# Where an attention kernel decodes the first dense layer's weights: four operations per engine in each of blocks 1 to 4, and dense products from block 5 on

## The chip, the core and the metric

One core of a Trainium2 chip runs the whole program. The metric is the device time of one execution in microseconds. The engines of the core run their own queues in order and meet through semaphores: TensorE (PE) multiplies and transposes, VectorE (DVE), ScalarE (ACT) and GpSimd (POOL) work on elements, SyncE (SP) issues the transfers.

## The reference, cut to what matters

The weight matrices arrive as float64 and reach the chip as raw 64-bit words. Three stages follow each other:

```python
# 1. attention, 2 batches x 8 heads, 768 positions, 64 per head; only 8 global keys and 96 local ones are kept
scores = q @ k.T / sqrt(64) - slope[h] * dist;  scores = where(keep, scores, -1e9)
x = softmax(scores) @ v                       # -> (2, 768, 512)
# 2. gated layer
h = relu(x @ w_in);  u, v = h[..., :512], h[..., 512:]
v_n = (v - mean(v)) / sqrt(var(v) + 1e-6)
v_s = w_spatial @ v_n + b_spatial             # over the 768 positions
x = (u * v_s) @ w_out
# 3. mixing layer
y = x + (x.T @ U @ V).T
out = y + relu(y @ w_ch1) @ w_ch2
```

## The kernel before

The kernel keeps everything of one batch in SBUF as two float32 halves, a rounded value (hi) and what is left (lo), and forms each product of the dense layers from three matmuls (`mm3`: hi hi, hi lo, lo hi).

The attention is a loop over `g`, the blocks of 128 queries: 12 of them (`NBL`), blocks 0 to 5 for the first batch and 6 to 11 for the second, and two more rounds to drain. It is pipelined over three rounds: block `g` computes its scores on PE (`em_s`), adds the bias on DVE (`em_soft`, which also finds the maximum), takes the exponential on ACT (`em_exp`) and scales on POOL (`em_norm`); the probabilities of block `g - 1` are transposed on PE (`em_t`, copied out of PSUM by ACT for even pairs of heads and by DVE for odd ones); those of block `g - 2` are multiplied with the values (`em_pv`) and written to `X` as hi and lo (`em_x`). The four pairs of heads of a block are its four pair steps `r`. Block 0's scores are taken before the masks and the bias for later blocks are finished.

Dense work that doesn't need the attention any more is put between these steps. It stands in a list, `fillers`, and `fill(more)` (line 659) takes `more` entries from it at each pair step: none in blocks 0 to 3, one in blocks 4 to 10, four from block 11 on (line 519; `TWO`, line 468, is 10). An entry is one step of three matmuls: first the four steps of each of six row tiles of `x @ w_in` for the half called `v` (`s_m1_v`, 24 entries, accumulated over the four chunks `k` of 128 rows; entry `k` needs chunk `k` of the weights), added from block 2 on, one tile per block; then 48 steps of the spatial product (`s_m2`), added at the end of block `TWO - 1`. From that block on the transposes use one PSUM bank instead of two, since the spatial product uses the other. What is left of `fillers` when the loop ends is taken behind it, together with the first product of the second batch.

Everything on DVE, ACT, POOL and SP that only prepares such work (decoding the weights from 64-bit words, splitting into hi and lo, loading `w_spatial`, layer normalisation) is not written at a fixed place but in chains, and a planner decides where it goes. The planner (class `Plan`) keeps for each engine the time at which it would be free by prices of its own. At certain points the program calls `tick` (line 162): it goes through the chains and emits the next operation of each for which the engine is free within `ROOM` (400 ns) of PE's own time and which needn't wait for more than `STALL` (100 ns); while `plan.most` is 1 (during the attention), at most one for each engine in a call. `flush` emits chains at once, whatever the planner thinks. There are two calls of `tick` in a pair step: behind the transposes and at its end; and one in each dense step.

The decoding of `w_in`'s `v` half consists of four chains (`early_work`, line 671), one for each chunk of 128 x 512 weights: an Abs on ACT; a clamp, a shift and two merging steps on DVE (`decode`, line 276); a rounding on ACT to `win` hi; a subtraction on POOL to `win` lo (`splits`, line 264). Their raw words are loaded at the start, into `rawin`, `masks` and `stg`. The first dense step calls `flush(P["wv"])`, that is, whatever of the four chains has not been emitted by then goes out at that point. Behind these chains come the load of `b_spatial` and those of `w_spatial` with their splits, which the spatial product needs.

Three small DVE operations on the counts of global and local keys and four that set a flag (`o_counts`, `o_flag`) form a chain of their own that is added at the end of block 0. The flag tells whether a second, dense program has to run after the first; with these inputs it doesn't.

Of the kernel before, what the change touches and what calls it, by code (L numbers as in the profile page):

```python
# [40 lines left out]
ROOM, CALM, STALL = 400.0, 450.0, 100.0  # L41
# [24 lines left out]
class Plan:  # L66
# [92 lines left out]
        if not c.ops:  # L159
            self.chains.remove(c)  # L160

    def tick(self):
        now, more, count = self.free["T"], True, dict.fromkeys(LAG, 0)
        while more:
            more = False
            for c in sorted(self.chains, key=lambda c: c.calm):
                key = c.ops[0][0]
                if any(d.ops for d in c.after) or self.free[key] > now + (CALM if c.calm else ROOM):
                    continue
                if self.most and count[key] >= self.most:  # L170
                    continue
                self.probing = 0.0
                c.ops[0][1]()
                start, self.probing = self.probing, None
                if start <= max(now, self.free[key]) + STALL:
                    count[key] += 1
                    self.emit(c)
                    more = True
# [14 lines left out]
def kernel(ctx: ExitStack, tc: tile.TileContext, qk, qt, kn, vab, vn_, gl_,  # L193
# [11 lines left out]
    def body(dense, sb, pp):  # L205
        plan = Plan(nc)
# [141 lines left out]
        if not dense:  # L348
# [116 lines left out]
                                        op0=ALU.mult, op1=ALU.mult)  # L465


            TWO = 10

            def em_t(g, r):  # L470
                x, bk = prob(g, r), bank[7 if g < TWO - 1 and r % 2 else 4].rearrange("p (h c q) -> p h c q", h=2, c=2)
# [25 lines left out]
            def attention():  # L497
                for e in range(2):
                    o_load(0, e)[0][1]()
                o_vals(0)[0][1]()  # L500
                A.activation(out=sm[:, 12:13], in_=nc.const_aps.tensor(0.0, (128, 1)), func=AF.Exp)
                V.memset(bank[4], 0.0)
                V.memset(bank[7], 0.0)
                masks_before()
                make_identity(nc, ident)
                for e in range(2):
                    o_load(1, e)[0][1]()
                early_work([t_x11[:, 0:1536], t_x11[:, 1536:3072], t_x10[:, 1536:3072], stg[:, 0:1536]])
                o_vals(1)[0][1]()
                plan.most = 1  # L510
                masks_first()
                masks_second()
                masks_third()
                for h in range(5, 8):
                    bias_g(Bt, rel, mk, h)


                for g in range(NBL + 2):
                    more = 0 if g < 4 else 1 if g < TWO else 1 if g == TWO else 4
                    if g == NB:  # L520
                        second_x()
                    xs = None
                    if g < NBL:
                        for r in range(NP):
                            em_s(g, r)
                        if g + 2 < NBL:
                            for e in range(2):
                                o_load(g + 2, e)[0][1]()
                    if g >= 2:
                        em_pv(g - 2)  # L530
                        if g < NBL:
                            o_vals(g)[0][1]()
                        xs = em_x(g - 2)
                    if g < NBL:
                        if g == 0:
                            for h in range(2, 4):
                                o_bias(B0, d0, m1, h)[1]()
                        em_soft(g, 0)
                        em_exp(g, 0)
                    if 0 < g <= NBL:  # L540
                        em_norm(g - 1, 1)
                    if g < NBL:
                        em_soft(g, 1)
                        em_exp(g, 1)
                        if g == 0:
                            for h in range(4, 8):
                                o_bias(B0, d0, m1, h)[1]()
                    if xs:
                        xs[0]()
                    for r in range(NP):  # L550
                        if xs and r == 1:
                            xs[1]()
                        if 0 < g <= NBL:
                            em_t(g - 1, r)
                            tick()
                        fill(more)
                        if g < NBL:
                            if r < 2:
                                em_soft(g, 2 + r)
                                em_exp(g, 2 + r)  # L560
                            if r == 1:
                                em_norm(g, 0)
                        tick()
                    if g == 0:
                        for h in range(5):
                            o_bias(Bt, rel, mk, h)[1]()
                        plan.add([("V", f) for f in o_counts() + o_flag()])
                    if 2 <= g < NB + 2:
                        fillers.extend(s_m1_v(0, g - 2, 6))
                    if g == NBL - 1:  # L570
                        plan.most = 0
                    if g == TWO - 1:
                        fillers.extend(s_m2(0, 6))

# [473 lines left out]
```

## Time and profile before

| what | value |
|---|---|
| three timed runs | 540.84, 541.87, 541.72 us; median 541.72 |
| profiled execution | 541.09 us, span from first to last instruction 539.3 us |
| mean granted clock of PE | 0.982 of 2.4 GHz |
| busy in the span | PE 506.0 us, DVE 305.6, ACT 213.5, POOL 176.0 |
| transfers | 44.74 MB, 83 GB/s in the mean |

The profiled execution is 0.6 us below the median; what is worked out from its rows is set against its own time. In the page's slices (13.5 us each) a digit is the busy share in tenths, and the row of the granted clock says at which share of 2.4 GHz PE was allowed to run. Views used are: the slices of the page, the list of PE's waits, single engines in order of time, groups of instructions by shape, and the busy time of each engine in chosen stretches. Nearly all instructions have the planner's line, L56, so they are told apart by their tiles: `raw` are the inputs of the scores, `prob` the probabilities, `ptb` their transposes, `win` the weights of the first layer, `wsp` those of the spatial product, `sm` small numbers.

### The profile page before, as it was taken

Reading aid. Unit: us, or ns where it says so; the run is one execution under the profiler, and the core shown is the slowest. Engines: PE = TensorE matmul, PEld = TensorE weight load, DVE = VectorE, ACT = ScalarE, POOL = GpSimd, SP = SyncE. Lnnn points to the kernel's source line nnn. Section 1 sums busy time; section 2 is a strip of 40 time slices with the busy share of each in tenths; the row PEclk is TensorE's granted clock in tenths of the full one; section 3 lists DMA queues with packets and bytes.
Section 4 is the critical chain, followed back from the end, with each engine's and each line's share of the span. In section 5 each row is a group of like instructions: output and inputs, shape, how many; then the busy total and the mean of one; then the engine's idle time right before and its main releaser. Section 6 shows DMA issues by size and latency. Waiting matters only on the chain.

```text
span 539.3 us, 7978 instructions
## 1 busy us (share of the span) xinstructions
PE 506.0 (94%) x2916; PEld 447.9 (83%) x2916; DVE 305.6 (57%) x734; ACT 213.5 (40%) x513; POOL 176.0 (33%) x207
## 2 busy tenths in 40 slices
PE   5847999799989999999999999999999999999994
PEld 3636877689869999888989898998988989989893
DVE  8777788753589963498699777685131111011113
ACT  4865977632253311564453433423212122121220
POOL 5526756430134401140024424233133232332310
PEclk9886999999999999999999999999999999999999
DMA  8772563130221210431215423420020000000003
GB/s 304 252 217 78 160 237 97 46 112 1 65 92 40 61 52 1 157 97 60 79 28 205 157 89 146 137 97 1 0 105 13 1 1 1 1 0 1 0 3 122
DMA packets 13520, 44.74 MB, mean 83 GB/s; under 512 B 1568, under 2 KB 3744, under 8 KB 11424
## 3 DMA queue, kind: packets, MB, share of 16 engines
q1 hardware_dynamic: 13328, 44.14, 24.3%
q8 instruction: 25, 0.41, 0.3%
q14 instruction: 23, 0.19, 0.1%
q10 hardware_dynamic: 144, 0.00, 0.0%
HBM read 40.99 MB, written 3.15 MB: 82 GB/s over the span
## 4 chain that ended last, share of the span: by engine, by line
PE 79%; DVE 11%; ACT 5%; issue 2%; DMA 1%; POOL 1%; ACTq 0%; SPq 0%; DVEq 0%
PE bank L56 79%; DVE stg L56 3%; DVE sm L56 2%; DVE prob L56 1%; ACT prob L56 1%; DVE y L56 1%; ACT ptb L56 1%; DVE u L56 1%; DMA stg<-in_w_in_dram 1%; DVE vn L56 1%; DMA ni<-in_gl_dram 1%; ACT stg L56 1%; DVE bias L56 1%; DVE work L56 1%; ACT x L56 0%
## 5 line engine op out<-in xcount | busy, mean ns | idle before, releaser
L56 POOL TENSOR_TENSOR wch<-f,wch 128x512 fp32r<-128x512 f32 x64 | 86.3, 1368 | 213.2 <-ACT wch L56 213.2
L56 PE MATMUL bank<-wch,h 128*128 128x512 f32 x576 | 139.4, 396 | 0.0
L56 PE MATMUL bank<-x,wch 128*128 128x384 f32 x768 | 139.1, 336 | 0.0
L56 PEld LDWEIGHTS bank<-x,wch 128*128 128x128 f32 x768 | 134.5, 188 | 3.1
L56 PEld LDWEIGHTS bank<-wch,h 128*128 128x128 f32 x576 | 107.8, 188 | 23.3
L56 DVE SCALAR_TENSOR_TENSOR h<-bank,h 128x384 fp32r<-128x384 f32 x64 | 35.5, 555 | 141.5 <-ACT h L56 141.5
L56 ACT ACTIVATE h<-bank 128x384 fp32r<-128x384 f32 x64 | 31.5, 492 | 179.5 <-PE bank L56 179.5
L56 ACT ACTIVATE prob<-prob,sm 128x232 f32<-128x232 f32 (+1 forms) x96 | 44.4, 464 | 29.1 <-DVE sm L56 29.1
L56 PE MATMUL bank<-wsp,vn 128*128 128x384 f32 x288 | 54.7, 341 | 1.1 <-POOL vn L56 0.3
L56 POOL TENSOR_SCALAR prob<-prob,sm 128x232 f32<-128x232 f32 (+1 forms) x96 | 43.4, 470 | 36.4 <-ACT prob L56 24.2
L56 PEld LDWEIGHTS bank<-wsp,vn 128*128 128x128 f32 x288 | 49.2, 188 | 2.8 <-DVE u L56 0.9
L56 PE MATMUL bank<-win,x 128*128 128x512 f32 x144 | 41.4, 422 | 9.9 <-ACT win L56 8.4
L56 DVE TENSOR_SCALAR f<-f 128x512 f32<-128x512 f32 (+1 forms) x64 | 41.3, 683 | 9.5 <-ACT f L56 9.3
L56 DVE SCALAR_TENSOR_TENSOR f<-raw,f 128x512 int32<-128x512 int32 x64 | 43.9, 725 | 0.1
L56 PEld LDWEIGHTS bank<-win,x 128*128 128x128 f32 x144 | 26.3, 197 | 14.6 <-ACT win L56 8.7
L56 ACT ACTIVATE wch<-f 128x512 fp32r<-128x512 f32 x64 | 36.9, 625 | 1.0 <-DVE f L56 1.0
L56 PE MATMUL bank<-x,win 128*128 128x384 f32 x192 | 34.2, 337 | 2.2 <-ACT win L56 1.3
L56 PE MATMUL bank<-ident,prob 128*128 128x128 f32 (+1 forms) x176 | 28.9, 287 | 7.2 <-ACT ptb L56 5.7
L56 PEld LDWEIGHTS bank<-x,win 128*128 128x128 f32 x192 | 33.2, 188 | 2.9 <-ACT win L56 1.7
L56 PE MATMUL bank<-wo,x 128*128 128x512 f32 x144 | 35.3, 395 | 0.0
L56 PEld LDWEIGHTS bank<-ident,prob 128*128 128x128 f32 (+1 forms) x176 | 20.7, 140 | 16.0 <-POOL prob L56 7.2
L56 DVE CUSTOM_DVE_ANT_0 prob<-bank,bias 128x232 f32<-128x232 f32 (+1 forms) x96 | 31.7, 369 | 2.6 <-PE bank L56 2.6
(87 smaller groups left out, 499.2 us busy)
## 6 DMA issues: line engine op xcount, KB each, us to landing
raw<-in_w_ch_dram SPq DMA_DIRECT2D x16, 1024.0 KB, 4.8
raw<-in_qk_dram SPq DMA_DIRECT2D x20, 360.0 KB, 3.8
vals<-in_vab_dram SPq DMA_DIRECT2D x10, 512.0 KB, 4.3
out_dram<-y SPq DMA_DIRECT2D x12, 256.0 KB, 2.2
stg<-in_w_in_dram SPq DMA_DIRECT2D x5, 512.0 KB, 5.9
stg<-in_w_sp_dram SPq DMA_DIRECT2D x3, 768.0 KB, 4.5
stg<-in_w_out_dram SPq DMA_DIRECT2D x4, 512.0 KB, 3.8
raw<-in_qk_dram SPq DMA_DIRECT2D x4, 256.0 KB, 3.6
```

Source lines behind the costliest of these rows:

```text
L56: return f(*a, **kw)
```

## The change

In the attention the constant `FILL` is new: dense steps are taken from block 5 on instead of 4, one per pair step through block 11 (`TWO` is 11 instead of 10), four from block 12 on. The tick at the end of each pair step of blocks 1 to 4 gets a room of 4000 ns instead of 400, and as a call with a larger room it also accepts an operation that would wait for up to 4000 ns. The chain on the counts and the flag is added at the end of block 11 (`NBL - 1`) instead of block 0. No operation is added or removed; the order of the instructions in each engine's queue changes.

```diff
--- before.py
+++ after.py
@@ -159,20 +159,20 @@
         if not c.ops:
             self.chains.remove(c)
 
-    def tick(self):
+    def tick(self, room=ROOM):
         now, more, count = self.free["T"], True, dict.fromkeys(LAG, 0)
         while more:
             more = False
             for c in sorted(self.chains, key=lambda c: c.calm):
                 key = c.ops[0][0]
-                if any(d.ops for d in c.after) or self.free[key] > now + (CALM if c.calm else ROOM):
+                if any(d.ops for d in c.after) or self.free[key] > now + (CALM if c.calm else room):
                     continue
                 if self.most and count[key] >= self.most:
                     continue
                 self.probing = 0.0
                 c.ops[0][1]()
                 start, self.probing = self.probing, None
-                if start <= max(now, self.free[key]) + STALL:
+                if start <= max(now, self.free[key]) + (STALL if room == ROOM else room):
                     count[key] += 1
                     self.emit(c)
                     more = True
@@ -465,7 +465,7 @@
                                         op0=ALU.mult, op1=ALU.mult)
 
 
-            TWO = 10
+            FILL, TWO = 5, 11
 
             def em_t(g, r):
                 x, bk = prob(g, r), bank[7 if g < TWO - 1 and r % 2 else 4].rearrange("p (h c q) -> p h c q", h=2, c=2)
@@ -516,7 +516,7 @@
 
 
                 for g in range(NBL + 2):
-                    more = 0 if g < 4 else 1 if g < TWO else 1 if g == TWO else 4
+                    more = 0 if g < FILL else 1 if g <= TWO else 4
                     if g == NB:
                         second_x()
                     xs = None
@@ -560,15 +560,15 @@
                                 em_exp(g, 2 + r)
                             if r == 1:
                                 em_norm(g, 0)
-                        tick()
+                        tick(4000.0 if 0 < g < FILL else ROOM)
                     if g == 0:
                         for h in range(5):
                             o_bias(Bt, rel, mk, h)[1]()
-                        plan.add([("V", f) for f in o_counts() + o_flag()])
                     if 2 <= g < NB + 2:
                         fillers.extend(s_m1_v(0, g - 2, 6))
                     if g == NBL - 1:
                         plan.most = 0
+                        plan.add([("V", f) for f in o_counts() + o_flag()])
                     if g == TWO - 1:
                         fillers.extend(s_m2(0, 6))
```

## Rows read from the trace of the kernel before

**Rows 1.** The page's 40 slices: busy tenths of PE, its granted clock

```profile
PE   5847999799989999999999999999999999999994
...
PEclk9886999999999999999999999999999999999999
```

**Rows 2.** What PE waited for, whole span: total us, times, longest us

```profile
PE bank L56 <- ACT win L56: 9.8, 2, 8.4
```

**Rows 3.** PE in order of time: start us, us, operation xcount [idle before <-releaser]

```profile
42.07 0.80 PE L56 MATMUL bank<-win,x 128*128 128x512 f32 x1 [8.44 <-ACT win L56]
...
46.08 1.63 PE L56 MATMUL bank<-win,x 128*128 128x512 f32 x3
...
54.80 0.94 PE L56 MATMUL bank<-win,x 128*128 128x512 f32 x3
...
59.10 1.16 PE L56 MATMUL bank<-raw 64*128 64x128 f32 x16
```

**Rows 4.** DVE in order of time in the burst, columns as in rows 3

```profile
36.92 0.75 DVE L56 TENSOR_SCALAR rawin<-rawin 128x512 int32<-128x512 int32 x2
...
37.59 0.42 DVE L56 TENSOR_SCALAR masks<-masks 128x512 int32<-128x512 int32 x1
...
38.26 1.28 DVE L56 SCALAR_TENSOR_TENSOR rawin<-rawin 128x512 int32<-128x512 int32 x2
...
39.46 0.68 DVE L56 SCALAR_TENSOR_TENSOR masks<-masks 128x512 int32<-128x512 int32 x1
```

**Rows 5.** Groups by shape, 34 to 48.1 us: busy us, mean ns, idle

```profile
L56 ACT ACTIVATE masks<-masks 128x512 f32<-128x512 f32 x1 | 0.7, 666 | 0.0
```

**Rows 6.** DVE in order of time, the marks of blocks 1 to 5

```profile
14.31 0.42 DVE L56 COPY ptb<-bank 128x256 f32<-128x256 f32 x1
...
17.87 0.40 DVE L56 CUSTOM_DVE_ANT_0 prob<-bank,bias 128x232 f32<-128x232 f32 x1 [1.42 <-PE bank L56]
...
27.32 0.69 DVE L56 TENSOR_TENSOR x<-bank,x 128x512 fp32r<-128x512 f32 x1 [0.62 <-ACT x L56]
...
30.39 0.40 DVE L56 CUSTOM_DVE_ANT_0 prob<-bank,bias 128x232 f32<-128x232 f32 x1 [0.27 <-PE bank L56]
...
52.28 0.37 DVE L56 CUSTOM_DVE_ANT_0 prob<-bank,bias 128x232 f32<-128x232 f32 x1
```

**Rows 7.** ACT in order of time, block 1

```profile
15.74 0.47 ACT L56 ACTIVATE prob<-prob,sm 128x232 f32<-128x232 f32 x1
```

**Rows 8.** DVE in order of time, two operations beside POOL

```profile
62.09 0.88 DVE L56 TENSOR_TENSOR wsp<-stg,wsp 128x512 fp32r<-128x512 f32 x1
...
97.24 1.12 DVE L56 SCALAR_TENSOR_TENSOR sm<-sm 128x3 f32<-128x3 f32 x1
```

**Rows 9.** POOL in order of time, a scaling of four and a subtraction

```profile
23.32 1.76 POOL L56 TENSOR_SCALAR prob<-prob,sm 128x232 f32<-128x232 f32 x4 [2.50 <-ACT prob L56]
...
97.07 1.27 POOL L56 TENSOR_TENSOR vn<-u,vn 128x512 fp32r<-128x512 f32 x1
```

**Rows 10.** Stretch: us, busy PE, PEld, DVE, ACT, POOL, then PEclk, DMA, GB/s

```profile
15.00:16.00 1.00, 0.97 (x6) 0.67 (x6) 0.62 (x6) 1.00 (x5) 0.18 (x1) 0.59 1.04 406
...
22.89:29.30 6.41, 5.92 (x65) 4.87 (x64) 5.44 (x26) 5.70 (x20) 3.51 (x8) 1.00 0.68 211
...
91.76:102.73 10.97, 8.23 (x77) 6.62 (x76) 8.47 (x33) 6.98 (x23) 6.78 (x13) 1.00 0.14 49
...
96.60:101.63 5.03, 2.29 (x15) 1.71 (x15) 3.97 (x16) 3.47 (x12) 2.61 (x6) 1.00 0.30 104
...
118.59:130.75 12.16, 12.16 (x97) 11.61 (x97) 3.47 (x6) 1.76 (x3) 1.01 (x3) 1.00 0.01 2
...
155.40:174.80 19.40, 17.22 (x98) 16.58 (x97) 18.55 (x31) 8.85 (x17) 9.57 (x7) 1.00 0.22 71
```

**Rows 11.** PE in order of time, at the attention's end and behind it

```profile
132.66 6.51 PE L56 MATMUL bank<-wsp,vn 128*128 128x384 f32 x36
...
158.45 0.62 PE L56 MATMUL bank<-x,win 128*128 128x384 f32 x2 [1.34 <-ACT win L56]
```

## The prediction

> **What bounds the kernel now.** I read the page's slices first: from the fifth of 40 on, TensorE's (PE's) row is almost all nines, so what can still be won lies in the first tenth, where the granted clock also falls to 0.6 of full speed [rows 1]. Then the waits of PE: the largest is not for a transfer but for ScalarE (ACT) writing `win`, 9.8 us in two waits [rows 2]. Then PE in order of time around it: it idles for 8.44 us, from 33.63 to the first dense product at 42.07, and three of these products then take 1.63 us at 46 us, against 0.94 us at 55 us [rows 3]; the idle PE had lost its clock. Then VectorE (DVE) and ACT in that hole: the decoding of the first layer's four weight chunks runs there in one burst, four Abs on ACT, sixteen steps on DVE, roundings on ACT and subtractions on GpSimd (POOL) [rows 4, 5]. The planner had put none of it into blocks 0 to 3; the first dense product, in block 4, flushes it. Last, DVE's marks: it takes the scores of blocks 2, 4 and 5 at 17.87, 30.39 and 52.28 [rows 6], so an undisturbed block lasts (30.39 - 17.87) / 2 = 6.26 us, and block 4 lasts 21.9.
>
> **What the change does to blocks 1 to 4.** It takes the four dense steps (12 matmuls) out of block 4, and lets the tick at the end of each of the 4 x 4 pair steps emit one operation for each of ACT, DVE and POOL with up to 4 us of lead. DVE has 4 chunks x 4 = 16 decoding steps, one for each such tick, so all fit by the end of block 4. ACT gets the four Abs in block 1, then a rounding whenever a chunk's last DVE step is out (two in block 2, one each in 3 and 4); POOL gets a subtraction behind each rounding.
>
> DVE's steps, per block: two that start 0.33 us apart and two 0.60 us apart, 1.87 us [rows 4].
> - Block 1: the first step waits for the first Abs, which stands on ACT where the exponential of 15.74 stands now [rows 7]. With 0.67 for the Abs [rows 5] DVE gets on at 16.4 instead of 14.31 [rows 6]: 2.1 us, and 1.87 for the steps, less the 1.42 us that DVE waits for PE in front of the scores of block 2 [rows 6]. Cost 2.5 us.
> - Blocks 2 to 4: DVE has two holes in such a block, 0.62 us before the subtraction on `x` (it waits for ACT) and 0.27 us before the next scores (for PE) [rows 6]. A block's first step (0.33) fits into the first; the second closes, since PE is ahead once DVE is the later engine. 1.87 - 0.33 - 0.27 = 1.27 us. ACT's rounding lies beside this and costs nothing while DVE is last; without that cover it is about an Abs, 0.67 us [rows 5], per block.
> - The steps now run beside POOL's normalisation, which they did not in the burst, and no row shows a decoding step beside POOL. The nearest: a DVE subtraction took 0.88 us beside POOL's scaling, where a step of that size takes 0.68 [rows 4, 8], and an operation on three numbers took 1.12 us [rows 8] while POOL ran a subtraction of 1.27 [rows 9]. Bounds per block: nothing (all in the gaps between POOL's operations), and 2.5 us (three steps held for 0.44 each, a quarter of POOL's 1.76 for four scalings, and one held for 1.12); a gain is excluded, as waiting shortens nothing. I take 0.5 us, by the first of the two rows (0.2 for each step that meets POOL, some two or three of four), as POOL is busy for 3.51 of 6.41 us in a block [rows 10].
>
> That makes 2.5 + 3 x 1.77 = 7.8 us more in the four blocks. Without any of it DVE would take the scores of block 5 at 30.39 + 6.26 = 36.7; with it at 44.5, where it is 52.28 now.
>
> **What that is worth.** The mark that I compare is PE's score matmuls of block 6, now at 59.10 [rows 3]: from there on PE is the bound on both sides. Block 5 has its four dense steps as now; from its scores on DVE to the next block's on PE it is 59.10 - 52.28 = 6.8 us now, and as PE will be ahead of DVE by then I take 6.4: 50.9. Block 4's four dense steps are still owed there, 4 x 0.78 = 3.1 us (0.94 less what the next matmul overlaps). Gain: 59.10 - 50.9 - 3.1 = 5.1 us; with the bounds of the contention 6.6 and -0.9, and 1 us either way for the mark.
>
> **The later blocks.** The ramp moves by one block: block 10 gets a dense step of the first layer per pair, block 11 a step of the spatial product per pair, 12 and 13 sixteen each, and 12 of the 48 are left for the time behind the attention. Block 10 now idles PE for 10.97 - 8.23 = 2.7 us [rows 10]; block 11 inherits that with the same softmax work: 0. Behind the attention the other half of the weights is decoded, and PE waits for it at 158 us (1.34 [rows 11], and 19.40 - 17.22 = 2.2 in that stretch [rows 10]). After the change that decoding is in the planner's list while the 12 left-over steps run, 6.5 us of PE (36 matmuls in 6.51 [rows 11]), and begins by as much earlier against PE's work; DVE has room, it works 3.47 of 12.16 us in the stretch before [rows 10]. A lead of 6.5 us covers a wait of 2.2: I take 1.9, bounds 0 (a chunk's buffer comes free too late) and 2.7. The seven small operations on the counts leave DVE's queue in blocks 2 to 4 and go to block 12, where DVE idles: 0, and 1 us if that cover is gone. The loads of `b_spatial` and `w_spatial` on SP, queued behind the decoding, go out one block later and are used one block later: 0, and a wait in block 11 of no more than the 2.7 us above again if they are late.
>
> Sum: 5.1 + 1.9 = 7.0 us. The profiled run took 541.09 us (span 539.3): 534.1. The median of the three runs is 541.72, 0.6 above it, so I forecast 534.7.
>
> **The rivals.**
> - *The port.* Every decoding step is held by a whole POOL operation: 2.5 us per block instead of 0.5, 6 us less gain: 540.7. For it: the 1.12 us. Against it: POOL is idle for nearly half of a block. The Trainium skill, "SBUF — State Buffer", section "Who interferes with whom", says that a VectorE operation with two SBUF inputs, or in a two-port mode, and a GpSimd operation that reads SBUF shut each other out for the whole of the one that began first. By that rule alone, with DVE always second, the time would be these 540.7; the 0.88 for 0.68 bears the rule out in kind, not in that size.
> - *The clock, the case that ends slower.* PE works 5.92 of 6.41 us in a block now [rows 10]; in one of 8.0 us that is 74%, with a hole of some 1.5 us while it waits for copies out of `bank`. If the clock falls to its lower level (1.2 GHz) in each, PE's work grows by 1.63 / 0.94 = 1.73 [rows 3] to 10.3 us, PE becomes the bound from 8.0 on, and 3 x 2.3 = 6.9 us go, with 2 more in block 5 until it recovers: 1.9 us slower, 543.6. For it: after PE had idled before 15.0 us the clock stood at 0.59 in the next [rows 10]. Against it: from 96.60 to 101.63 PE worked 2.29 of 5.03 us at 1.00 [rows 10]. The Trainium skill, "TensorE: Matmul & The Clock Gate", section "What's actually happening", calls the slow clock the resting state that activity lifts; which of the two this share of activity is, only the 1.00 row tells, and it was enough there.
> - *Not all sixteen fit.* In block 1 ACT stands some 4 us ahead of PE, about the new limit, so some operations slip and are flushed by the first dense product. With half of the burst's 8.44 us left the gain falls by some 3 us (DVE's share of it is owed anyway): 537.7.
> - *Given back.* The gain in front is real, but DVE ends block 11 and PE idles there as much longer: 541.7.
>
> **How the numbers follow.** Forecast 0.70 (531 to 538), better than that (no contention, both late waits gone) 0.06, not all sixteen 0.06, port 0.06, given back 0.04, clock 0.08. About 0.2% (1.1 us) is what a measurement here can tell from no change. Range 530 to 540: the forecast's, the third rival and most of the better case, 0.82. Faster: 0.70 + 0.06 + 0.06 and most of the port's = 0.87; same 0.05; slower 0.08.
>
> **What would show it.** Right: no wait of PE for `win` before 50 us; DVE takes the scores of block 2 at about 20.3 and of block 5 at 44.5; four decoding steps per block; clock 1.00 from 22 us on; no wait for `win` behind the attention. Wrong: DVE steps of over 1 us beside POOL (port); clock near 0.5 in blocks 2 to 4; a burst of steps at the first dense product; longer waits of PE in blocks 10 and 11. The step that I trust least is the 0.5 us per block.

## The result, and the profile after

| kernel | median us | lowest to highest | of before, 95% interval |
|---|---|---|---|
| before | 541.79 | 540.84 to 541.87 | |
| after | 533.81 | 532.87 to 535.09 | 0.9858 [0.9835, 0.9882] |

The forecast was 534.7 with a range of 530 to 540; the change is 8.0 us faster. The profiled run of after took 532.87 us (span 531.1), 8.2 less than that of before. The sum said 7.0. So the time is right to a microsecond, and the question is whether it is so for the reasons given.

The 40 slices of the page of after, PE and its granted clock, stand against [rows 1]: PE is busy for 6 and 8 tenths of the third and fourth slices (27 to 53 us) where it was 4 and 7, and the clock there, 8 and 6 before, is 9 and 8.

```profile
PE   5768999799999999999999999999999999999994
...
PEclk9998999999999999999999999999999999999998
```

The chain of waits that ended last runs through PE for 88% of the span (79% before) and through DVE for 8% (11%):

```profile
PE 88%; DVE 8%; ACT 1%; issue 1%; DMA 1%; POOL 0%; ACTq 0%
```

What PE waited for in after (us in total, times, longest us). Of the 9.8 us for ACT's `win` [rows 2] nothing is left, neither the 8.44 in front nor the 1.34 behind the attention; in their place there are two waits of 2.3 us for POOL's `prob`. The first lines:

```profile
PE bank L56 <- DMA raw<-in_qk_dram: 4.9, 1, 4.9
PE bank L56 <- POOL prob L56: 4.6, 2, 2.3
PE bank L56 <- ACT ptb L56: 4.4, 4, 1.7
```

DVE of after in order of time (start us, us, operation, in brackets the idle time before it and what ended it), for [rows 6]. The operations with `bias` are the first scores of blocks 2, 3, 4 and 5: 19.77, 28.40, 36.34 and 44.72, where 20.3 and 44.5 were forecast for the first and the last. All sixteen steps on `rawin`, `masks` and `stg` stand ahead of 44.72. They are not four to a block, though: three stand before 19.77, and five, five and three between these marks. The wide ticks of block 1 gave three, and in each of blocks 2 to 4 the ordinary tick behind the first transposes gave one.

```profile
16.32 0.43 DVE L56 TENSOR_SCALAR rawin<-rawin 128x512 f32<-128x512 f32 x1 [2.02 <-ACT rawin L56]
...
18.57 0.68 DVE L56 SCALAR_TENSOR_TENSOR rawin<-rawin 128x512 int32<-128x512 int32 x1
19.77 0.40 DVE L56 CUSTOM_DVE_ANT_0 prob<-bank,bias 128x232 f32<-128x232 f32 x1 [0.52 <-PE bank L56]
...
25.53 1.65 DVE L56 SCALAR_TENSOR_TENSOR rawin<-rawin 128x512 int32<-128x512 int32 x1
...
28.40 0.39 DVE L56 CUSTOM_DVE_ANT_0 prob<-bank,bias 128x232 f32<-128x232 f32 x1
...
36.34 0.38 DVE L56 CUSTOM_DVE_ANT_0 prob<-bank,bias 128x232 f32<-128x232 f32 x1
...
36.97 1.03 DVE L56 TENSOR_SCALAR sm<-sm 128x4 f32<-128x4 f32 x1
...
44.72 0.40 DVE L56 CUSTOM_DVE_ANT_0 prob<-bank,bias 128x232 f32<-128x232 f32 x1 [0.99 <-PE bank L56]
```

ACT of after, same columns. Behind the last copy of block 4 stands the first rounding of `w_spatial`, in front of block 5's exponentials, and it waits for its load:

```profile
44.93 0.63 ACT L56 ACTIVATE wsp<-stg 128x512 fp32r<-128x512 f32 x1 [0.65 <-DMA stg<-in_w_sp_dram]
```

POOL of after, same columns, for [rows 9]: the subtraction that the 1.65 and the one that the 1.03 met, and a scaling of four that takes 2.63 us instead of 1.76.

```profile
25.10 1.53 POOL L56 TENSOR_TENSOR win<-rawin,win 128x512 fp32r<-128x512 f32 x1 [1.73 <-ACT win L56]
26.61 2.63 POOL L56 TENSOR_SCALAR prob<-prob,sm 128x232 f32<-128x232 f32 x4
...
36.71 1.27 POOL L56 TENSOR_TENSOR win<-masks,win 128x512 fp32r<-128x512 f32 x1
```

PE of after, same columns, for [rows 3]. The first dense product comes at 47.94, with no wait before it. The scores of block 5 (16 matmuls at 42.77) take 2.92 us where those of block 4 take 1.84; those of block 2, at 17.82, take 3.45. The mark of the forecast, the scores of block 6, stands at 52.22, with four dense steps done and four owed, as planned; 50.9 was forecast.

```profile
17.82 3.45 PE L56 MATMUL bank<-raw 64*128 64x232 f32 x16
...
32.13 0.62 PE L56 MATMUL bank<-ident,prob 128*104 128x128 f32 x4 [2.30 <-POOL prob L56]
...
33.70 1.84 PE L56 MATMUL bank<-raw 64*128 64x232 f32 x16
...
40.77 0.61 PE L56 MATMUL bank<-ident,prob 128*104 128x128 f32 x4 [2.31 <-POOL prob L56]
41.78 1.06 PE L56 MATMUL bank<-ident,prob 128*104 128x128 f32 x4 [0.39 <-DVE ptb L56]
42.77 2.92 PE L56 MATMUL bank<-raw 64*128 64x232 f32 x16
...
47.94 0.95 PE L56 MATMUL bank<-win,x 128*128 128x512 f32 x3
...
52.22 1.16 PE L56 MATMUL bank<-raw 64*128 64x128 f32 x16
...
150.41 16.81 PE L56 MATMUL bank<-x,win 128*128 128x384 f32 x96
167.07 8.14 PE L56 MATMUL bank<-wsp,vn 128*128 128x384 f32 x46
```

The last two lines answer [rows 11]: 96 matmuls in one unbroken 16.81 us, where before two were followed by a wait and the rest came after a second one.

Stretches of after (us, busy PE, PEld, DVE, ACT, POOL, then the granted clock, DMA share and GB/s). Of the three blocks between the marks the third has a mean clock of 0.81: it stood at 0.50, the lower of its two levels (1.2 GHz, of 2.4), from 42 to 44, and recovered in the next two. At the beginning the row can't be taken at its word: it reads 1.00 while the scores of block 2 run at about half of the speed of block 4's.

```profile
18.00:19.00 1.00, 1.00 (x6) 0.90 (x8) 1.00 (x4) 1.00 (x5) 0.83 (x2) 1.00 0.00 0
...
19.77:28.40 8.63, 8.15 (x86) 6.43 (x86) 8.53 (x29) 6.80 (x22) 6.39 (x10) 1.00 0.64 187
28.40:36.34 7.94, 5.23 (x54) 4.01 (x52) 7.84 (x29) 6.58 (x21) 6.38 (x11) 1.00 0.42 121
36.34:44.72 8.38, 5.68 (x48) 4.57 (x44) 7.33 (x27) 6.18 (x20) 6.07 (x10) 0.81 0.82 265
...
42.00:44.00 2.00, 2.00 (x10) 1.57 (x10) 1.70 (x6) 1.88 (x6) 1.25 (x3) 0.50 0.95 390
44.00:46.00 2.00, 2.00 (x18) 1.56 (x18) 1.28 (x5) 1.35 (x5) 2.00 (x4) 0.75 0.06 17
```

Where the 8.2 us came from, by marks on PE with the same work behind them in both traces:

| up to | before | after | gained in this stretch |
|---|---|---|---|
| scores of block 6 | 59.10 | 52.22 | 3.8, after 3.1 for the four steps owed |
| first dense product of the second batch | 139.01 | 134.06 | 1.2 (4.95 in all) |
| first product with the second half of `win` | 155.38 | 150.41 | 0.0 |
| second spatial product | 174.75 | 167.07 | 2.7 |
| first product of the second batch with the second half of `win` | 200.53 | 192.03 | 0.8 |
| end of the run | 541.09 | 532.87 | -0.3 |

The 1.2 of the second line is a wait of 1.12 us of PE for a copy of `ptb` in block 8, at 80.71 in before, that isn't there in after. Block 11 of after waits 1.46, 0.84 and 0.79 us, 3.1 in all, where block 10 of before waits 1.13, 0.82 and 0.78: as forecast, this goes along to the next block unchanged.

### The profile page after: what moved, and what is told of

It reads as the page before. It is cut to its first block, busy times and chain, and to the rows that moved or that the text cites. A ratio compares the mean times of both kernels' runs of the same rounds, so it can differ in the third digit from the quotient of the medians.

```text
span 531.1 us, 7975 instructions
## 1 busy us (share of the span) xinstructions
PE 504.7 (95%) x2916; PEld 447.5 (84%) x2916; DVE 304.6 (57%) x734; ACT 213.0 (40%) x513; POOL 180.8 (34%) x207
## 4 chain that ended last, share of the span: by engine, by line
PE 88%; DVE 8%; ACT 1%; issue 1%; DMA 1%; POOL 0%; ACTq 0%
PE bank L56 88%; DVE prob L56 2%; DVE sm L56 1%; DVE rawin L56 1%; DVE y L56 1%; DVE ptb L56 1%; DMA ni<-in_gl_dram 1%; DVE masks L56 1%; DVE bias L56 1%; ACT prob L56 1%; DVE x L56 0%; ACT ptb L56 0%; ACT vn L56 0%; POOL vn L56 0%; DVE stg L56 0%
## 5 line engine op out<-in xcount | busy, mean ns | idle before, releaser
L56 POOL TENSOR_SCALAR prob<-prob,sm 128x232 f32<-128x232 f32 (+1 forms) x96 | 47.2, 509 | 32.0 <-ACT prob L56 24.4
L56 PE MATMUL bank<-wsp,vn 128*128 128x384 f32 x288 | 53.2, 339 | 0.9 <-DVE vn L56 0.4
L56 PE MATMUL bank<-win,x 128*128 128x512 f32 x144 | 39.1, 406 | 0.0
L56 PE MATMUL bank<-raw 64*128 64x232 f32 (+1 forms) x192 | 26.7, 423 | 5.6 <-DMA raw<-in_qk_dram 4.9
```

The lines of the kernel that those rows point to most:

```text
L56: return f(*a, **kw)
```

## Experiments

The change has two parts that can be had alone: the room that lets the planner emit four steps per block, and the shift of the ramp of dense steps by one block.

**The shift alone: e1_shift_only.** Ordinary ticks, and the seven operations on the counts back in their old place; `FILL` and `TWO` as in after.

```diff
-                        tick(4000.0 if 0 < g < FILL else ROOM)
+                        tick()
                     if g == 0:
                         for h in range(5):
                             o_bias(Bt, rel, mk, h)[1]()
+                        plan.add([("V", f) for f in o_counts() + o_flag()])
...
-                        plan.add([("V", f) for f in o_counts() + o_flag()])
```

> The changed kernel with the ordinary tick in blocks 1 to 4 and the counts at their old place: only the ramp of dense steps is moved by one block. Theory (two gains of their own: the front one needs the spreading, the late one the 12 left-over steps): the burst of sixteen decoding steps comes back one block later, PE idles 8 to 10 us for win in block 5, scores of block 6 at PE at about 57 us with 4 dense steps done (before: 59.1 with 8, that is 1 us worse), the wait for win near 155 us is gone (2.2 to 3 us better): 539.5, between 538 and 541. Rival (the move of the ramp alone is the gain, the room is nothing): 534.

Measured 538.42 us (537.84 to 538.94), 0.9931 [0.9917, 0.9945]. PE of this run in order of time: the burst is still there, whole, one block later, and behind the attention nothing is waited for.

```profile
49.43 0.79 PE L56 MATMUL bank<-win,x 128*128 128x512 f32 x1 [8.44 <-ACT win L56]
...
156.22 16.81 PE L56 MATMUL bank<-x,win 128*128 128x384 f32 x96
```

So the twelve left-over steps alone take away the late wait, and the shift is worth 3.5 us with the burst in place. My theory held.

**The room alone: e2_room_only.**

```diff
-            FILL, TWO = 5, 11
+            FILL, TWO = 4, 10
```

> The changed kernel with FILL 4 and TWO 10: dense steps as before, the wide tick in blocks 1 to 3 only, so 12 of 16 decoding steps are spread and the last chunk's four go out at the first dense step. Theory: no long wait of PE for win, as the first dense step needs chunk 0 alone; PE's scores of block 5 at about 44 us with 4 dense steps done (50.7 before), 6 to 7 us gained in front, and the waits for win near 155 us back (2 to 2.5 us): 535.5, between 534 and 537.5. Rival (the room is nothing without the move, since the flush holds PE anyway): 541.

Measured 536.72 us (535.52 to 538.21), 0.9905 [0.9887, 0.9922]. PE in order of time:

```profile
153.16 0.62 PE L56 MATMUL bank<-x,win 128*128 128x384 f32 x2 [1.30 <-ACT win L56]
154.62 15.02 PE L56 MATMUL bank<-x,win 128*128 128x384 f32 x85 [0.84 <-POOL win L56]
```

The burst is gone and the late waits are back. (With `FILL` at 4 only blocks 1 to 3 have wide ticks.) The two parts are worth 3.5 and 5.2 us, 8.7 in all, against 8.0 and 8.6 for the whole (after, and e5_again below): they are two separate gains, in two places of the trace, which nearly add.

**The shift of `TWO` taken back: e3_two10.** The decoding has its four blocks, the spatial product begins one block earlier, and nothing is left over.

```diff
-            FILL, TWO = 5, 11
+            FILL, TWO = 5, 10
```

> The changed kernel with TWO 10 (FILL 5 kept): all 48 steps of the spatial product fit into the attention again, so none are left to lie over the decoding behind it. Theory (the late gain is the lead of the left-over steps): PE waits for win behind the attention again, 1.5 to 2.5 us, partly paid back by block 11, where sixteen steps now lie under the softmax instead of four (its 3.1 us of waits fall to 1 to 2): 535, between 534 and 536.5. Rival (that wait went because everything in front of it came earlier): no such wait, 532 to 533.

Measured 538.18 us (536.88 to 542.07), 0.9937 [0.9917, 0.9957]. The waits for `win` behind the attention are back (1.34 and 0.84 us), as expected, but they are only half of the 4.4 us by which this is slower than after, and more than I expected. Two more things stand in the trace: the first spatial steps of block 11 wait 1.31 us for `vn`, and behind the late waits 85 matmuls take 16.57 us, which took 15.02 in the room alone; the clock is 0.58 from 156 to 160 us there. That it can fall behind the attention too was not in my expectation. The executions of this kernel lie 5 us apart, so the trace of one doesn't settle the size.

**POOL's subtraction kept away from the transposes: e4_hold_sub.** PE's two waits of 2.3 us end with POOL's `prob`. A subtraction of 1.3 us stands before the scalings on POOL. Here POOL gets nothing from the planner in the last pair step of these blocks.

```diff
-                        tick(4000.0 if 0 < g < FILL else ROOM)
+                        tick(4000.0 if 0 < g < FILL else ROOM, "G" if 0 < g < FILL and r == NP - 1 else None)
```

(in `tick`, a chain whose next operation is for the engine `skip` is passed over)

> The changed kernel, but the wide tick at the last pair step of blocks 1 to 4 emits nothing for POOL, so each subtraction on win stands behind the next block's first scaling instead of before it. Theory (POOL's order made PE late in blocks 3 and 4: 4.6 us of waits for prob, a clock at half from 42 to 45 us, and DVE waiting 0.99 us for PE in front of block 5): the waits for prob fall below 1 us, block 6's scores on PE at about 51 instead of 52.2, 1 us faster: 532.8. Rival (DVE is last in these blocks and the waits of PE only lie beside it): 533.8, unchanged.

Measured 533.53 us (533.08 to 534.31), 0.9843 [0.9827, 0.9858]: no change. PE's waits:

```profile
PE bank L56 <- ACT ptb L56: 9.3, 6, 2.6
PE bank L56 <- DMA raw<-in_qk_dram: 5.1, 1, 5.1
```

No wait for POOL is left, and the same holes stand there with ACT's copy as the releaser (2.62 and 2.31 us). My theory, that POOL was late, fell; PE takes the scores of block 6 at 53.87 in this trace, not at 51. Which engine is named is a matter of which of several late ones is last; DVE has no idle time in blocks 2 and 3 (8.53 of 8.63 and 7.84 of 7.94 us busy in after), all others wait for it, and PE's holes only show that PE is ahead.

**The same kernel again: e5_again**, unaltered, beside the next three.

> The changed kernel once more, unaltered, beside the three others of this call, since they are to be told from it by less than 0.3%: 533.8, between 533 and 535.

533.25 us (533.04 to 534.98), 0.9851 [0.9833, 0.9868]. DVE takes the scores of blocks 2 and 5 at 20.04 and 45.00, PE those of block 6 at 52.54.

**The counts back: e6_counts_back.** I had put the move of the seven small operations at nothing.

```diff
                         for h in range(5):
                             o_bias(Bt, rel, mk, h)[1]()
+                        plan.add([("V", f) for f in o_counts() + o_flag()])
...
-                        plan.add([("V", f) for f in o_counts() + o_flag()])
```

> The changed kernel with the seven small operations on the counts back at the end of block 0. Theory (their move is worth nothing, since DVE has both places to spare): within 0.5 us of the changed kernel, 533.8. Rival (they take DVE's turn in ticks of blocks 2 to 4 and push decoding steps beyond block 4): one to two steps and a rounding and subtraction are flushed at the first dense step, 1 to 2 us slower, 535.5.

Measured 532.15 us (530.86 to 533.39), 0.9826 [0.9809, 0.9842]: 1.1 us faster than after beside it, which neither expectation had (0.8 when it was run again, e12 below; the ranges of the executions overlap). DVE in order of time:

```profile
14.51 0.18 DVE L56 CAST sm<-ni 128x4 f32<-128x4 int32 x1
...
16.62 1.26 DVE L56 TENSOR_SCALAR rawin<-rawin 128x512 f32<-128x512 f32 x2 [0.68 <-ACT rawin L56]
...
18.73 0.39 DVE L56 CUSTOM_DVE_ANT_0 prob<-bank,bias 128x232 f32<-128x232 f32 x1
```

In after the first decoding step is DVE's operation in block 1's first wide tick, and DVE stands before it for 2.02 us until the Abs is out, with the copy, the scores and the sums of the last pair behind it. Here a count of 0.18 us takes that turn, the copy and the scores go first, the decoding step comes later and waits 0.68 us, and DVE gets to the scores of block 2 at 18.73 instead of 20.04. So by this trace it isn't the counts that matter, but what DVE had to do before a step that couldn't start.

**PE kept at work in the front: e7_busy_pe.** Transposes of the identity into an unused bank, behind the transposes of the second pair in blocks 1 to 4 (12 of them) and of the third pair in block 1 (10). This puts the clock to the test.

```diff
                             em_t(g - 1, r)
                             tick()
+                            for _ in range(12 if r == 1 and g < FILL else 10 if r == 2 and g == 1 else 0):
+                                nc.tensor.transpose(bank[6][:, 0:128], ident, ident)
```

> The changed kernel with idle work for PE in its holes in blocks 1 to 4: twelve transposes of the identity into a bank that nobody reads, behind the second pair's transposes, and ten more in block 1 behind the third's. Theory (the fall of the clock between 42 and 45 us in the changed kernel costs time, as PE's scores of block 5 take 2.92 us instead of 1.84 and DVE waits 0.99 for them): clock 1.00 up to 60 us, block 6's scores on PE at about 51 instead of 52.2, 1 us faster: 532.8. Rival (DVE is last there, and a slow PE is hidden): unchanged at 533.8, or up to 1 us slower where the idle work delays a transpose.

Measured 533.26 us (532.43 to 535.61), 0.9857 [0.9838, 0.9876], as after. In front the theory is borne out: the clock is 1.00 throughout, DVE no longer waits for PE before the scores of block 5 (43.49, 45.00 in after beside it), and PE's scores of block 6 come at 51.35 instead of 52.54. But not all of this is the fall between 42 and 45 us. A third of the 1.5 us at DVE's mark was won in block 1: block 2's scores take 1.84 us on PE here and 3.47 in after beside it, where DVE waits 0.52 us for them. And behind that mark something else holds the block. DVE waits for `x` from ACT, because ACT stands in front of the rounding of `w_spatial` until the load is there (PE, ACT and DVE of this run):

```profile
17.80 1.84 PE L56 MATMUL bank<-raw 64*128 64x232 f32 x16
...
45.32 0.63 ACT L56 ACTIVATE wsp<-stg 128x512 fp32r<-128x512 f32 x1 [1.20 <-DMA stg<-in_w_sp_dram]
...
48.36 0.69 DVE L56 TENSOR_TENSOR x<-bank,x 128x512 fp32r<-128x512 f32 x1 [2.60 <-ACT x L56]
```

Of the 1.2 us at block 6's scores, 0.7 are left at block 11's (91.84 against 92.56) and 0.3 behind the attention (134.03 against 134.33); what goes last goes in block 11. Stretches of this run there:

```profile
96.00:100.00 4.00, 1.84 (x12) 1.23 (x10) 3.93 (x14) 2.94 (x12) 2.75 (x5) 0.95 0.74 253
100.00:104.00 4.00, 3.89 (x22) 3.26 (x24) 1.74 (x11) 1.53 (x5) 1.76 (x4) 0.62 0.35 142
```

PE idles for over half of 96 to 100 us, and in the next four the clock is 0.62 on average; in after beside it the clock is 1.00 there, and by the end of that block PE is only 0.3 us later than here (117.74, here 117.44).

**The ramp of before with twelve steps left over: e8_ramp4_left12.** If the two gains add, one can have the earlier ramp of the room alone and keep the lead at the end.

```diff
-            FILL, TWO = 5, 11
+            FILL, TWO = 4, 10
...
-                    more = 0 if g < FILL else 1 if g <= TWO else 4
+                    more = 0 if g < FILL else 1 if g <= TWO else 2 if g == TWO + 1 else 3
```

> The front of the room-only kernel with left-over steps for the time behind the attention: dense steps from block 4 on, wide ticks in blocks 1 to 3, one step of the spatial product per pair in block 10, two in block 11, three in blocks 12 and 13, so that 12 of 48 are left. Theory (front and late gain are two things and add up): the front as there (5.2 us by block 10), the late waits for win gone (2.5 us), block 11 idle for 0 to 1 us more: 534, between 533 and 535. Rival (the late lead is worth nothing without the later ramp): 536.7.

Measured 536.19 us (534.67 to 538.42), 0.9896 [0.9876, 0.9916]: 2 us more than expected. The waits for `win` are gone, but block 11, with 8 spatial steps, takes 15.8 us, as long as it does with 16 in before (102.73 to 118.59 [rows 10]):

```profile
97.60:113.40 15.80, 13.67 (x91) 11.34 (x90) 10.76 (x36) 7.33 (x22) 4.78 (x9) 0.78 0.31 101
```

It waits three times for `vn` (0.71, 0.68 and 0.61 us), and the clock is 0.78. With fewer dense steps in it the block is, by this trace, bound by the layer normalisation and by a PE that is slowed down in its holes. I read from it that the left-over steps are only worth their lead if nothing idles where they are taken from.

**POOL's scaling left out: e9_no_scaling.** This kernel leaves out POOL's scaling of the probabilities in blocks 1 to 4, so that the decoding steps have nothing beside them but the subtractions.

```diff
-                for r in range(2 * e, 2 * e + 2):
+                for r in range(2 * e, 2 * e + 2) if not 1 <= g <= 4 else ():
```

> The changed kernel without POOL's scaling of the probabilities in blocks 1 to 4 (32 operations left out, so those blocks' attention is not divided by its sums): POOL has only the four subtractions there. Theory (the decoding steps and the small operations on DVE are held up by POOL, 0.9 us a block by the changed kernel's trace against the 0.5 of the forecast, and the transposes no longer wait for prob): decoding steps at 0.43, 0.42, 0.68, 0.68 us but for those beside a subtraction, blocks 2 to 4 each 0.5 to 0.9 us shorter, scores of block 5 on DVE at 42 to 43 instead of 45.0: 531, between 530 and 532.5. Rival (DVE's own work makes the block and POOL costs nothing): 533.3, unchanged.

Measured 533.49 us (532.11 to 535.28), 0.9855 [0.9828, 0.9882]. DVE in order of time:

```profile
25.23 1.37 DVE L56 TENSOR_SCALAR rawin<-rawin 128x512 int32<-128x512 int32 x1
26.64 0.69 DVE L56 SCALAR_TENSOR_TENSOR rawin<-rawin 128x512 int32<-128x512 int32 x1
...
43.73 0.40 DVE L56 CUSTOM_DVE_ANT_0 prob<-bank,bias 128x232 f32<-128x232 f32 x1 [0.69 <-PE bank L56]
```

The steps are back at 0.42 and 0.69, but for the two that meet a subtraction (1.37 at 25.23, 0.83 at 29.99). DVE takes block 5's scores at 43.73 instead of 45.00 and PE those of block 6 at 51.55 instead of 52.54: that gives the contention with the scaling as 1 us for the three blocks in front. In the total no gain can be told from the scatter; 531 was expected. The clock stood at 0.66 from 40 to 44 us here too.

**The first step one tick later: e10_skip_first.** This tests the reading of e6: DVE gets nothing in block 1's first wide tick, and the counts stay where after has them.

```diff
-                        tick(4000.0 if 0 < g < FILL else ROOM)
+                        tick(4000.0 if 0 < g < FILL else ROOM, "V" if (g, r) == (1, 0) else None)
```

> The changed kernel, but the first wide tick of block 1 emits nothing for DVE, so the first decoding step stands behind pair 3's scores; the counts stay at the end of block 11 and one step is left for block 5. Theory (what made the kernel with the counts back 1.1 us faster is that its first count takes this turn, so that DVE waits 0.68 instead of 2.02 us for the first Abs): scores of block 2 at 18.7 instead of 20.0 on DVE, 532.2. Rival (the counts' place itself brought it): 533.3.

Measured 532.58 us (531.63 to 537.65), 0.9836 [0.9813, 0.986]. DVE of its profiled run:

```profile
16.63 1.18 DVE L56 TENSOR_SCALAR rawin<-rawin 128x512 f32<-128x512 f32 x2 [0.77 <-ACT rawin L56]
...
18.66 0.39 DVE L56 CUSTOM_DVE_ANT_0 prob<-bank,bias 128x232 f32<-128x232 f32 x1
```

The mark is that of e6 (18.73): the place of the first step decides, not the counts. The profiled run is the slowest of the six, 537.65. The clock was 0.55 from 32 to 38 us in it, but DVE still has block 5's scores at 42.96, where e6 has them at 43.00. The time is lost behind that mark, to the load of `w_spatial` (ACT and PE of this run):

```profile
48.23 0.63 ACT L56 ACTIVATE wsp<-stg 128x512 fp32r<-128x512 f32 x1 [4.64 <-DMA stg<-in_w_sp_dram]
...
51.85 1.07 PE L56 MATMUL bank<-ident,prob 128*104 128x128 f32 x4 [4.06 <-ACT ptb L56]
```

PE idles, works at a clock of 0.50 from 51 to 56 us, and takes the scores of block 6 at 56.26 instead of 51.26. The load was issued at 39.89 (38.72 in e6); whether the slow clock before it made it late isn't shown.

**Both together: e11_filled**, and **e12_counts_back_2**, which is e6_counts_back once more beside it. e11 has the edit of e6, the transposes of e7, and more of them in block 11 (8, 5 and 5 in its first three pair steps).

```diff
                         fill(more)
+                        if g == TWO:
+                            for _ in range((8, 5, 5, 0)[r]):
+                                nc.tensor.transpose(bank[7][:, 384:512], ident, ident)
```

> The kernel with the counts back, and idle transposes on PE in the holes of blocks 1 to 4 and of block 11 (12 and 10 as before; 8, 5 and 5 behind the first three steps of the spatial product). Theory (each fall of the clock costs 0.5 to 1.2 us, and the gain of the filled front was lost to a fall in block 11): clock 1.00 up to 170 us, 531, between 530.3 and 531.8. Rival (holes filled are holes no longer there to catch up in): 532.2, as without.

> The kernel with the counts back once more, unaltered, beside the two kernels of this call that are to be told from it: 532.2, between 531 and 533.4.

| kernel | median us | lowest to highest | of before, 95% interval |
|---|---|---|---|
| e11_filled | 531.58 | 530.55 to 531.64 | 0.9808 [0.9791, 0.9826] |
| e12_counts_back_2 | 532.46 | 530.84 to 535.39 | 0.9837 [0.981, 0.9864] |

The slices of e11's page, and the stretch that was slow in e7:

```profile
PE   5988999999999999999999999999999999999994
...
PEclk9999999999999999999999999999999999999998
```

```profile
100.00:104.00 4.00, 3.76 (x42) 3.24 (x42) 2.09 (x12) 1.53 (x5) 2.15 (x5) 1.00 0.27 110
```

e11_filled is the fastest kernel here by its median: its slowest execution (531.64) is below the fastest of after (532.87), with the kernel before at the same time beside both (541.92 and 541.79). Against the counts alone its median is 0.9 lower, less than their scatter, and the best executions are hardly apart (530.55 and 530.84). What differs is the upper end, 531.64 against 535.39: five executions within 1.1 us against six within 4.5. Whether the clock makes this difference isn't shown. It is 1.00 in the front and in block 11 of e11 and 0.58 from 40 to 44 us in e12, and yet block 6's scores come at 50.91 in e11 and at 50.74 in e12, and both spans are 529.6 us. In e11 too ACT waits for the load of `w_spatial`, 1.66 us (0.76 in e12). Only one execution of each has a trace.

## Why the prediction was right, step by step

- *Room for all sixteen steps.* Right: none left for the first dense product. That rival is out. But "four decoding steps per block" was wrong as a mark: by DVE's marks there are 3, 5, 5 and 3.
- *Block 1, 2.5 us.* It cost 19.77 - 17.87 = 1.9 us [rows 6]. The wait for the Abs was forecast as it came (2.02 us; 2.1 worked out), three steps instead of four stand before the mark, and DVE still waits 0.52 us there for PE's slow scores. What I didn't see is that it could have been avoided: by e6 and e10 1.3 us of it is the place of the step in DVE's queue.
- *Blocks 2 to 4, 1.27 + 0.5 us each.* From mark to mark they take 24.95 us, forecast 3 x 8.03 = 24.1; but 0.99 of it is DVE's wait for PE at the end, so DVE's own time, 23.96, is as forecast. Three errors hide in this. These blocks hold thirteen of the steps, not twelve. The contention was larger: against the same operations alone the held ones take about 1.1, 0.7 and 0.9 us more in the three blocks (0.97 of it at 25.53, 0.86 at 36.97), so 0.9 a block instead of 0.5; some 0.2 of it stand in before's blocks too, where the same small operation takes 0.47 us once (at 24.62). And the holes closed wholly: I had counted 0.60 of the 0.89 us per block as filled, and DVE has none left.
- *The port as a rival.* In kind it is there and in size it is not: 0.9 us a block, not 2.5. The Trainium skill, "SBUF — State Buffer", section "Who interferes with whom", lets the operation that comes second wait for the whole of the first; that fits the worst cases (1.65 us beside a subtraction of 1.53, 1.03 for an operation on four columns beside one of 1.27), and POOL pays as well (2.63 instead of 1.76 us for four scalings). What keeps the sum small, as I read the trace, is that most of the sixteen steps met no more than the end of a short operation.
- *"PE will be ahead of DVE by then", 6.4 us from DVE's mark in block 5 to PE's in block 6.* This step failed. It took 52.22 - 44.72 = 7.5 us. At its mark DVE waited 0.99 us for PE: PE had been ahead in blocks 3 and 4, idled (2.31 us before 40.77), and then did four transposes and the scores of block 5 in 1.06 and 2.92 us instead of 0.62 and 1.84, most of it at a clock of 0.50; from 42.77 on it works without a hole. So the front gave 3.8 us, where 5.1 was the forecast. The clock is only a part of it: in e7, at 1.00, PE's mark comes 1.2 us earlier, but from DVE's mark to PE's it is 51.35 - 43.49 = 7.9 us.
- *The loads of `b_spatial` and `w_spatial`: 0, or a wait in block 11.* Wrong, and hidden in after. The first rounding of `w_spatial` stands in ACT's queue before its load is there, and block 5's exponentials and copies stand behind it. ACT waits 0.65 us for it in after, where PE is busy meanwhile, 1.20 in e7, 1.66 in e11, 1.78 in e6 and 4.64 in the slow execution of e10. Where block 4 has ordinary ticks (e2) it is 0.29, so I take it for a consequence of the wide tick there, which accepts an operation that has to wait. No run took this wait away; what it costs in the total is open.
- *The clock as a rival.* It fell at the end of block 4 and not in each block: 1.00 in blocks 2 and 3, with PE busy for 8.15 of 8.63 and 5.23 of 7.94 us. Block 2's scores, 3.45 us, were slow besides, at a recorded 1.00, and cost DVE 0.52 us. Together they cost 1.2 us at block 6's scores by e7, and not 8.9; in the medians of e7 and e5 (533.26 and 533.25) nothing of it is left. "Clock 1.00 from 22 us on" was wrong as a mark.
- *Block 11 inherits 2.7 us: 0.* Right (3.1 against 2.7). But block 8's 1.1 us, which went with the change, was in no term of mine. The wait of PE for ACT's copy in block 8 is 0.24 us or less where dense steps begin in block 5 (e1, e3), and 1.08 where they begin in block 4 (e2): it went with the shift. Why the shift shortens it isn't shown.
- *The late wait, 1.9 us.* Right in place (e1 and e2 switch it with the shift alone) and too small: the waits of 1.34 and 0.84 us, the 0.34 us for `u` behind them and some small holes go, 3.5 us in all (2.7 and 0.8 in the table of marks).
- *The counts, 0.* Wrong by about 1 us (1.1 by e6, 0.8 by e12): as the change makes it, it is a loss within the gain. The cover that I named, DVE's idle time in block 12, is there; what I missed is what took their place in DVE's queue in block 1.
- *Given back.* Out: nothing of the front's gain is lost up to 139 us.

In the sum: 3.8 + 1.2 + 3.5 - 0.3 = 8.2, against 5.1 + 1.9 = 7.0. The mechanism was right and both halves of it are shown apart; the front's term was 1.3 too large, the late one 1.6 too small, and a term of 1.2 was missing. That the total came within a microsecond owes something to that.

What stays open is, first, what the record of the clock says at the beginning of a trace. It reads 1.00 from 14 to 22 us of after, also where PE idles, and in that time the sixteen score matmuls of block 2 take 3.45 us; in before, with the clock recorded at 0.50 for the most part, they take 3.14, and in e7, with PE's hole filled, 1.84. So PE was slow there in after as well, whatever the row says. Second, what the wait for the load of `w_spatial` costs. And third, whether less contention in front would show in the total at all (e9), since its microsecond is as large as what the clock and that wait give and take there.

## What to carry to other kernels

A burst of preparing work in front of the first use of a buffer is worth spreading over earlier blocks even where the engine that does it is the bound there, as long as the consumer idles for the whole burst: the cost is the work itself and some contention, the gain is the idle time of the other engine and its clock. When an operation is put into an in-order queue ahead of its input, count everything behind it: here one step placed a tick too early cost more (1.3 us at the next mark) than the contention of a whole block, and a rounding placed ahead of its load held ACT for 0.65 to 4.64 us. And where TensorE is ahead and waits, its holes aren't always free: its clock can fall in them. Idle operations that keep it up there are worth a try, but here filling the front alone gave nothing in the total, and filling block 11 too gave a narrower spread in five executions, which is too few to build on.

## What the runs showed of the hardware that I had not expected

- The tensor engine's clock fell after some holes and not after others of the same length: in after the hole of 2.30 us before 32.13 us was followed by scores at full speed (1.84 us), the one of 2.31 us before 40.77 by scores at half (2.92 us). That this is what makes the times of one kernel differ (532.87 to 535.09 in after) isn't shown: in the slowest execution with a trace (e10, 537.65) PE's longest hole in block 5, 4.06 us, goes back to a load.
- The recorded clock and the speed of the matmuls can differ at the beginning of a trace: sixteen score matmuls took 3.45 us at a recorded 1.00 (17.82 in after), and 1.84 at 1.00 later (24.95). The time of one known matmul is the safer sign.
- Contention with POOL goes both ways and by whole operations: an operation on 128 x 4 numbers took 1.03 us beside a subtraction of 1.27, 0.17 elsewhere; and leaving out POOL's scaling brought DVE's steps back to 0.42 and 0.69 us at once, but for those beside a subtraction.
